# Attention's 64 left rows in full 128-partition tiles, in a kernel of linear attention and two MLPs

## The chip, the cores and the metric

The kernel runs on one core of one Trainium2 chip. The metric is the device time of one execution in microseconds (us); less is better. Matrix products and transpositions run on TensorE (PE; the loading of its stationary operand is shown as PEld), elementwise work on VectorE (DVE), ScalarE (ACT) and GpSimd (POOL), and SyncE (SP) issues most of the DMAs.

## The reference

Linear attention with a norm, then two MLPs on its output; all in float32 (the weights of the MLPs come as float64):

```python
kv  = einsum('bhsd,bhse->bhde', k, v)        # batch 4, heads 8, s 576, d 64
o   = einsum('bhsd,bhde->bhse', q, kv)
o   = o / sqrt(mean(o*o, -1) + 1e-6) * g_norm
x   = o.transpose(0, 2, 1, 3).reshape(2304, 512)
x   = softplus(x @ w_in)  @ w_out            # 512 -> 2048 -> 512
out = leaky_relu(x @ w_in2, 0.01) @ w_out2
```

## The kernel before, in words

**Units.** Attention is done in 16 units, one for two heads of one batch (4 batches, 4 pairs of heads). A batch has 576 rows, which are four full tiles of 128 partitions and 64 left rows. The full rows are loaded by unit (`load`, L363 to L373, five buffers deep), the left rows of all heads once for each batch (L377) into tiles of 64 partitions, `ldr`.

**One unit.** `T` (L383 to L429): GpSimd (in two cases another engine) repacks q and k (`copy_to`, L338); PE transposes the four q tiles (L400) and the left q rows (L404, 64 partitions, `ident[:RL, :RL]`) into PSUM, which is copied to `qt`, whose columns are 128, 128, 64 (left), 128, 128. PE then sums k-transposed times v over the four full tiles (L408) and the left rows (L411, contraction over 64 partitions); VectorE multiplies this with a mask into `kvm` (L426). `O` (L433 to L454): PE multiplies the four full tiles of `qt` with `kvm` (L439) and the 64 left columns (L445, an output of 64 partitions in `ps[6]`), and ACT and DVE take the sums of squares. For every second unit `normal` (L469 to L506) forms the norm and writes `xn` and, for the left rows, `xnl`. `X` (L517 to L545) transposes `xn` (L523) and, once for two units, `xnl` (L535, 64 partitions) and writes the result, scaled, to `xy`, the x of the MLPs.

A product in float32 is two passes on PE (two pairs of a weight load and a matmul in the trace), a transposition one.

**Order.** Nothing is issued in the order of the source: each piece of work is an `op` with a cost for each engine that may do it, with the buffers that it reads and writes, and `Plan.run` (L91 to L150) puts them into one fixed order for each engine from these costs and due times. The engines then work through their orders, each waiting by semaphores. The costs of PE in the plan are 0.25 for each half of the transpositions of q, 1.1 for kv, 0.87 and 0.22 for the two parts of `O`, 0.44 and 0.11 for those of `X`. The change leaves all of them.

**The MLPs** follow. Their first products (L888) stand among attention's last units; the rest (L813, L961, L977) fill the time behind attention. The decoding of the weights (L576 to L594) and their splitting (L610 to L669) for them is spread over ACT and DVE, during attention too.

Of the kernel before, what the change touches and what calls it, by code (L numbers as in the profile page):

```python
# [131 lines left out]
def linear_attention_two_mlps(  # L132
# [32 lines left out]
    nc = tc.nc  # L165
    B, H, S, D = q.shape
    NT, DM = out.shape
    DFF = w1.shape[1] // 2
    P = 128
    KC = DM // P  # L170
    NF = DFF // P
    RL = S - 4 * P
# [29 lines left out]
    def ring(pool, name, n, shape, dt=F32):  # L202
        return [pool.tile(shape, dt, name=f"{name}{i}") for i in range(n)]

    ident = const.tile([P, P], F32, name="ident")
# [91 lines left out]
    ps = ring(psum, "ps", 8, [P, 512])  # L297
# [3 lines left out]
    mstp = mst.__enter__()  # L301
    att = tc.tile_pool(name="att", bufs=1)
    attp = att.__enter__()
    NLD = 5
    lda = {nm: ring(attp, nm + "a", NLD, [P, 2, 4, D]) for nm in "qkv"}
    ldr = {nm: ring(attp, nm + "r", 2, [RL, H, D]) for nm in "qkv"}
    qp = ring(attp, "qp", 2, [P, 4, 2, D])
    kp = ring(attp, "kp", 2, [P, 4, 2, D])
    qt = ring(attp, "qt", 2, [P, S])
    kvm = ring(attp, "kvm", 2, [P, P])  # L310
    sq = ring(mstp, "sq", 2, [P, 8, D])
    sql = ring(mstp, "sql", 1, [RL, 4, D])
    xn = ring(mstp, "xn", 4, [P, 8, D])
    xnl = ring(mstp, "xnl", 2, [RL, 4, D])

    ss = ring(mstp, "ss", 2, [P, 20])
    fa = ring(mstp, "fa", 2, [P, 20])
    fm = ring(mstp, "fm", 2, [P, 20])
    for t_ in ss:
        nc.vector.memset(t_, 1.0)  # L320

    plan = Plan()
    op = plan.op
# [39 lines left out]
    def load(u):  # L363
        b, hp = u // NPAIR, u % NPAIR
        hs = slice(2 * hp, 2 * hp + 2)
        for nm, src in (("q", q), ("k", k), ("v", v)):
            def fn(e, nm=nm, src=src):
                nc.sync.dma_start(  # L368
                    out=lda[nm][u % NLD],
                    in_=src[b, hs, 0:4 * P, :].rearrange("h (p r) d -> p h r d", r=4),  # L370
                )

            op({"S": 0.73}, fn, (), [(nm, u % NLD)])  # L373
        if hp == 0:
            for nm, src in (("q", q), ("k", k), ("v", v)):
                def fn(e, nm=nm, src=src):
                    nc.sync.dma_start(  # L377
                        out=ldr[nm][b % 2], in_=src[b, :, 4 * P:S, :].rearrange("h p d -> p h d")
                    )

                op({"S": 0.73}, fn, (), [(nm + "r", b % 2)])

    def T(u):  # L383
        b, hp = u // NPAIR, u % NPAIR
        h2 = slice(2 * hp, 2 * hp + 2)
        i = u % 2
        for nm, dst in (("q", qp), ("k", kp)):
            copy_to(
                dst[i], lda[nm][u % NLD].rearrange("p h r d -> p r h d"), 512,
                [(nm, u % NLD)], [(nm + "p", i)],  # L390
            )
        p0 = 2 * i if u < U_H else 0
        p1 = p0 + 1
        kv = ps[p1][:, 2 * P:3 * P]
        ql, kl, vl = (ldr[nm][b % 2] for nm in "qkv")
        va = lda["v"][u % NLD]

        def f_t(e, j):
            for r in range(2):
                nc.tensor.transpose(  # L400
                    ps[p0 + j][:, r * P:(r + 1) * P], qp[i][:, 2 * j + r, :, :], ident
                )
            if j == 0:
                nc.tensor.transpose(ps[p0][:, 2 * P:2 * P + RL], ql[:, h2, :], ident[:RL, :RL])  # L404

        def f_kv(e):
            for r in range(4):
                nc.tensor.matmul(  # L408
                    kv, kp[i][:, r, :, :], va[:, :, r, :], start=(r == 0), stop=False
                )  # L410
            nc.tensor.matmul(kv, kl[:, h2, :], vl[:, h2, :], start=False, stop=True)  # L411

        for j in range(2):
            n = (2 * P + RL, 2 * P)[j]
            c0 = (0, 2 * P + RL)[j]
            op(
                {"PE": 0.25}, lambda e, j=j: f_t(e, j),
                [("qp", i)] + ([] if j else [("qr", b % 2)]), [("ps", p0 + j)],
            )
            if j:  # L420
                op(
                    {"PE": 1.1}, f_kv,
                    [("kp", i), ("v", u % NLD), ("kr", b % 2), ("vr", b % 2)], [("ps", p1)],
                )
                op(
                    {"D": 0.22}, lambda e: nc.vector.tensor_tensor(kvm[i], kv, mask, ALU.mult),  # L426
                    [], [("ps", p1), ("kvm", i)],
                )
            from_psum(qt[i][:, c0:c0 + n], ps[p0 + j][:, :n], n, p0 + j, [("qt", i, j)])  # L429
# [3 lines left out]
    def O(u):  # L433
        i = u % 2
        at_ = (0, P, 2 * P + RL, 3 * P + RL)

        def f_o(e):
            for r in range(4):
                nc.tensor.matmul(  # L439
                    ps[4 + i][:, r * P:(r + 1) * P], qt[i][:, at_[r]:at_[r] + P], kvm[i],  # L440
                    start=True, stop=True,
                )

        def f_l(e):
            nc.tensor.matmul(  # L445
                ps[6][:RL, i * P:(i + 1) * P], qt[i][:, 2 * P:2 * P + RL], kvm[i],
                start=True, stop=True,
            )

        need = [("kvm", i), ("qt", i, 0)]  # L450
        op({"PE": 0.87}, f_o, need + [("qt", i, 1)], [("ps", 4 + i)])
        op({"PE": 0.22}, f_l, need, [("ps", 6)])
        squares(ps[4 + i], ("ps", 4 + i), sq[i], ss[u // 2 % 2][:, 8 * i:8 * i + 8], ("sq", i),
                ("ss", u // 2 % 2, i), P, 8)  # L454
# [14 lines left out]
    def normal(w):  # L469
        i = w % 2  # L470
        s_, a_, m_ = ss[i], fa[i], fm[i]
        mk = [("fm", i)]
        sk, ak = [("ss", i, t) for t in range(3)], [("fa", i)]
        ol = ps[6][:RL, 0:2 * P]
        squares(ol, ("ps", 6), sql[0], s_[:RL, 16:20], ("sql", 0), sk[2], RL, 4)
        op(
            {"A": 0.2},
            lambda e: nc.scalar.activation(
                a_, s_, AF.Ln, bias=eps_b, scale=2.0 ** -SHIFT / D
            ), sk, ak,  # L480
        )
        op(
            {"A": 0.2},
            lambda e: nc.scalar.activation(a_, a_, AF.Exp, bias=ln_b, scale=-0.5),
            ak, ak + [("set", 0)],
        )

        def newton(e):
            nc.vector.scalar_tensor_tensor(m_, s_, D * EPS, a_, ALU.add, ALU.mult)
            nc.vector.scalar_tensor_tensor(m_, m_, 1.0 / D, a_, ALU.mult, ALU.mult)  # L490
            nc.vector.scalar_tensor_tensor(m_, m_, -3.0, a_, ALU.add, ALU.mult)

        op({"D": 0.55}, newton, sk + ak, mk)
        parts = [
            (xn[2 * i + t], ps[4 + t], m_[:, 8 * t:8 * t + 8], ("ps", 4 + t), ("xn", 2 * i + t), P, 8)
            for t in range(2)
        ] + [(xnl[i], ol, m_[:RL, 16:20], ("ps", 6), ("xnl", i), RL, 4)]
        for x_, o, r_, ok, xk, p, n in parts:
            op(
                {"D": t_d(n * D)},  # L500
                lambda e, x_=x_, o=o, r_=r_, p=p, n=n: nc.vector.tensor_tensor(
                    x_, o.rearrange("p (g d) -> p g d", d=D),
                    r_[:, :, None].to_broadcast([p, n, D]), ALU.mult,
                ),
                mk, [ok, xk],
            )  # L506
# [10 lines left out]
    def X(u):  # L517
        b, hp = u // NPAIR, u % NPAIR
        i = u % 2

        def f_x(e):
            for r in range(4):
                nc.tensor.transpose(  # L523
                    ps[7][:, r * P:(r + 1) * P], xn[u % 4][:, 2 * r:2 * r + 2, :], ident
                )

        cm, cl = (b * S + RL, b * S) if b % 2 else (b * S, b * S + 4 * P)
        op({"PE": 0.44}, f_x, [("xn", u % 4)], [("ps", 7)])
        scaled(xy[:, hp, cm:cm + 4 * P], ps[7], 4 * P, 7, xyk([hp], cm, 4 * P))
        if i == 0:  # L530
            return

        def f_l(e):
            for t in range(2):
                nc.tensor.transpose(  # L535
                    ps[6][:, 2 * P + t * RL:2 * P + (t + 1) * RL],
                    xnl[u // 2 % 2][:, 2 * t:2 * t + 2, :], ident[:RL, :RL],
                )

        op({"PE": 0.11}, f_l, [("xnl", u // 2 % 2)], [("ps", 6)])  # L540
        scaled(
            xy[:, hp - 1:hp + 1, cl:cl + RL],
            ps[6][:, 2 * P:2 * P + 2 * RL].rearrange("p (a n) -> p a n", a=2),
            2 * RL, 6, xyk([hp - 1, hp], cl, RL),
        )  # L545

# [473 lines left out]
    for t in range(2):  # L1020
        op(
            {"S": 0.1},
            lambda e, t=t: nc.sync.dma_start(
                out=graw[t * D:(t + 1) * D, :], in_=g_norm.rearrange("(p o) -> p o", o=1)
            ),
# [40 lines left out]
    for s in range(2 * NT2 + 2):  # L1066
        t, u = s // 2, s % 2
# [84 lines left out]
```

## Time and profile before

| | us |
|---|---|
| median of 3 runs (lowest, highest) | 844.09 (843.69, 844.68) |
| the profiled execution: its own time | 841.17 |
| its span, first to last instruction | 839.4 |
| PE busy / DVE busy / ACT busy / POOL busy | 824.8 / 578.1 / 447.8 / 65.6 |

The profile is one execution. Its rows give the start of a piece of work from the start of the span in us, its length, the engine, the line of the kernel, and what it reads and writes. "x8" is eight instructions in one row. PE's matmuls are pipelined: the busy time of one overlaps that of the next, so the distance at which they follow one another is read from the chain of waits, whose pieces lie end to end. Attention takes about the first 93 us of the span; the MLPs have the rest.

### The profile page before, as it was taken

The numbers are of one execution on the slowest core, as the hardware profiler recorded it, in microseconds if no ns is written. First come the engines' busy times: TensorE is split into PE (matmuls) and PEld (weight loads), VectorE is DVE, ScalarE is ACT, GpSimd is POOL, SyncE is SP. The second block draws the span as 40 slices with busy tenths as digits, with TensorE's granted clock in tenths as the row PEclk, the third lists the DMA queues.
The fourth block names the chain that finished last, engine by engine and source line by source line (L and its number), as shares of the span: only waits on it lengthen the run. The fifth ranks groups of instructions, "written<-read, shape, count | busy, mean of one in ns | idle before, by whom it ended". The sixth has DMA issues, their size and how long they took to land.

```text
span 839.4 us, 11949 instructions
## 1 busy us (share of the span) xinstructions
PE 824.8 (98%) x4524; PEld 772.0 (92%) x4524; DVE 578.1 (69%) x928; ACT 447.8 (53%) x725; POOL 65.6 (8%) x116
## 2 busy tenths in 40 slices
PE   6999999999999999999999999999999999999997
PEld 4788999999999999999999988989889889889886
DVE  6887988878468665867688886766378754753342
ACT  4644976866355544555466565565364554453330
POOL 3321000000100100000000000010010010010000
PEclk9999999999999999999999999999999999999999
DMA  9981565376645752764866965764654852543613
GB/s 309 342 271 64 201 244 188 145 251 211 222 135 162 248 204 72 249 202 158 302 209 212 324 252 191 253 221 134 210 168 135 286 176 65 200 152 100 200 51 100
DMA packets 78712, 164.08 MB, mean 195 GB/s; under 512 B 11456, under 2 KB 54208, under 8 KB 78656
## 3 DMA queue, kind: packets, MB, share of 16 engines
q1 hardware_dynamic: 67136, 100.42, 35.7%
q0 software_dynamic: 11520, 62.92, 22.6%
q8 instruction: 35, 0.57, 0.3%
q14 instruction: 21, 0.17, 0.1%
HBM read 132.25 MB, written 31.06 MB: 195 GB/s over the span
## 4 chain that ended last, share of the span: by engine, by line
PE 96%; DVE 1%; DMA 1%; ACT 1%; SPq 0%; issue 0%; ACTq 0%; DVEq 0%
PE ps L813 40%; PE ps L961 24%; PE ps L977 24%; PE ps L439 2%; PE ps L408 2%; PE ps L888 2%; PE ps L400 1%; PE ps L523 1%; DMA qr<-in_q_dram 1%; PE ps L411 1%; PE ps L445 1%; PE ps L404 0%; DVE xy L691 0%; PE ps L535 0%; SPq L368 0%
## 5 line engine op out<-in xcount | busy, mean ns | idle before, releaser
L813 PE MATMUL ps<-ra 128*128 128x384 f32 x1932 | 387.8, 335 | 0.0
L813 PEld LDWEIGHTS ps<-ra 128*128 128x128 f32 x1932 | 342.8, 188 | 14.0
L961 PE MATMUL ps<-rb 128*128 128x384 f32 x1152 | 226.6, 334 | 0.0
L977 PE MATMUL ps<-rb 128*128 128x512 f32 x864 | 224.7, 393 | 0.0
L961 PEld LDWEIGHTS ps<-rb 128*128 128x128 f32 x1152 | 202.1, 188 | 0.0
L921 DVE TENSOR_TENSOR mf<-ps,mf 128x384 f32<-128x384 f32 x138 | 76.7, 556 | 165.6 <-PE ps L813 134.3
L977 PEld LDWEIGHTS ps<-rb 128*128 128x128 f32 x864 | 159.8, 188 | 23.7
L914 ACT ACTIVATE mf<-ps 128x384 f32<-128x384 f32 x138 | 67.8, 492 | 109.4 <-PE ps L813 108.2
L691 DVE TENSOR_TENSOR xy<-ps,xy 128x384 f32<-128x384 f32 (+1 forms) x126 | 77.3, 614 | 29.1 <-PE ps L977 20.8
L796 POOL DMA_DIRECT2D ra<-xscr x80 | 42.8, 536 | 672.3 <-PE ps L813 652.8
L847 DVE TENSOR_TENSOR rb<-mf,rb 128x768 fp32r<-128x768 f32 x96 | 91.3, 951 | 3.9 <-ACT rb L842 3.8
L842 ACT ACTIVATE rb<-mf 128x768 fp32r<-128x768 f32 x96 | 81.3, 847 | 2.7
L719 ACT ACTIVATE ra<-mf 128x768 fp32r<-128x768 f32 x63 | 53.0, 841 | 27.7 <-PE ps L813 26.7
L714 DVE TENSOR_TENSOR ra<-mf,ra 128x768 fp32r<-128x768 f32 x63 | 60.1, 955 | 11.0 <-ACT ra L719 10.7
L834 ACT ACTIVATE mf<-mf 128x768 f32<-128x768 f32 (+1 forms) x48 | 32.8, 683 | 61.6 <-DVE mf L921 61.6
L828 ACT ACTIVATE mf<-mf 128x768 f32<-128x768 f32 (+1 forms) x48 | 33.3, 694 | 45.1 <-DVE mf L921 45.0
L686 ACT ACTIVATE xy<-ps 128x384 f32<-128x384 f32 (+1 forms) x35 | 18.5, 528 | 15.1 <-PE ps L961 10.8
L588 DVE SCALAR_TENSOR_TENSOR sqr<-mf,sqr 128x512 int32<-128x512 int32 x35 | 24.4, 696 | 0.8
L594 DVE SCALAR_TENSOR_TENSOR mf<-mf,sqr 128x512 int32<-128x512 int32 x34 | 24.0, 706 | 0.4
L576 ACT ACTIVATE mf<-mf 128x512 f32<-128x512 f32 x20 | 13.4, 669 | 17.1 <-DMA mf<-in_moe_w_in_dram 13.7
L400 PE MATMUL ps<-ident,qp 128*128 128x128 f32 x64 | 13.3, 306 | 8.6 <-POOL qp L347 7.8
L582 DVE TENSOR_SCALAR sqr<-mf 128x512 int32<-128x512 int32 x34 | 15.4, 453 | 8.1 <-ACT mf L576 7.5
(85 smaller groups left out, 606.6 us busy)
## 6 DMA issues: line engine op xcount, KB each, us to landing
ra<-xscr POOLq DMA_DIRECT2D x80, 768.0 KB, 6.0
mf<-xscr SPq DMA_DIRECT2D x51, 384.0 KB, 5.5
mf<-in_moe_w_in_dram SPq DMA_DIRECT2D x18, 512.0 KB, 4.8
xscr<-ra SPq DMA_DIRECT2D x12, 768.0 KB, 3.8
xscr<-rc SPq DMA_DIRECT2D x12, 768.0 KB, 4.6
mf<-in_moe_w_out_dram SPq DMA_DIRECT2D x17, 512.0 KB, 4.3
lf<-in_moe_w_out_dram SPq DMA_DIRECT2D x15, 512.0 KB, 3.5
xscr<-xy SPq DMA_DIRECT2D x19, 384.0 KB, 4.1
```

The lines of the kernel that those rows point to most:

```text
L691: {"D": t_d(n)}, lambda e: nc.vector.tensor_tensor(dst, src, dst, ALU.add),
L714: ENG[e].tensor_tensor(e_[:, 1, :, :], src(), e_[:, 0, :, :].bitcast(F32), ALU.subtract)
L719: {"A": t_a(n)}, lambda e: nc.scalar.activation(e_[:, 0, :, :], src(), AF.Copy),
L796: lambda e: nc.gpsimd.dma_start(out=flat(xe[i]).ap, in_=xscr[7 * tp + i]),
L813: nc.tensor.matmul(o, w_[:, a, c:c + P], e_[:, b, kk, :], start=(not on and kk == 0 and n == 0), stop=(kk == 1 and n == 2), skip_group_che ...
L828: {"A": t_a(n)}, lambda e: nc.scalar.activation(dst(), src(), AF.Softplus),
L842: {"A": t_a(n)}, lambda e: nc.scalar.activation(g[:, 0, :, :], c.ap, AF.Copy),
L847: lambda e: nc.vector.tensor_tensor(g[:, 1, :, :], c.ap, g[:, 0, :, :].bitcast(F32), ALU.subtract),
L914: {"A": t_a(BN)}, lambda e: nc.scalar.activation(c[:, m, :], src, AF.Copy),
L921: lambda e: nc.vector.tensor_tensor(c[:, m, :], src, c[:, m, :], ALU.add),
L961: nc.tensor.matmul(y[:, :BN], w_[m][:, a, js], G_[:, b, m, :], start=(u == 0 and m == 0 and i == 0), stop=(u == 1 and m == 1 and i == 2),)
L977: nc.tensor.matmul(y, G_[:, a, m, js], w_[m][:, b, :], start=(u == 0 and m == 0 and i == 0), stop=(u == 1 and m == 1 and i == 2),)
```

## The change

The tiles of the left rows (`ldr` for q, k, v, and `xnl`) get 128 partitions instead of 64. The lower 64 are set to zero once, ahead of everything else, by eight memsets on VectorE; the DMAs and the norm write the upper 64 as before. The transposition of the left q rows, the kv product of the left rows and the transposition of `xnl` take all 128 partitions. The left product of `O` takes 128 columns of `qt` (the 64 left ones and the first 64 of the next tile) and writes 128 partitions of `ps[6]`, of which 64 are read; for this it needs the second half of `qt` too. The copies out of PSUM take the same elements as before.

```diff
-    ldr = {nm: ring(attp, nm + "r", 2, [RL, H, D]) for nm in "qkv"}
+    ldr = {nm: ring(attp, nm + "r", 2, [P, H, D]) for nm in "qkv"}
...
-    xnl = ring(mstp, "xnl", 2, [RL, 4, D])
+    xnl = ring(mstp, "xnl", 2, [P, 4, D])
...
+    for t_ in [t for n in "qkv" for t in ldr[n]] + xnl:
+        nc.vector.memset(t_[RL:], 0.0)
     for t_ in ss:
         nc.vector.memset(t_, 1.0)
...
-                        out=ldr[nm][b % 2], in_=src[b, :, 4 * P:S, :].rearrange("h p d -> p h d")
+                        out=ldr[nm][b % 2][:RL], in_=src[b, :, 4 * P:S, :].rearrange("h p d -> p h d")
...
-                nc.tensor.transpose(ps[p0][:, 2 * P:2 * P + RL], ql[:, h2, :], ident[:RL, :RL])
+                nc.tensor.transpose(ps[p0][:, 2 * P:3 * P], ql[:, h2, :], ident)
...
-                ps[6][:RL, i * P:(i + 1) * P], qt[i][:, 2 * P:2 * P + RL], kvm[i],
+                ps[6][:, i * P:(i + 1) * P], qt[i][:, 2 * P:3 * P], kvm[i],
...
-        need = [("kvm", i), ("qt", i, 0)]
-        op({"PE": 0.87}, f_o, need + [("qt", i, 1)], [("ps", 4 + i)])
+        need = [("kvm", i), ("qt", i, 0), ("qt", i, 1)]
+        op({"PE": 0.87}, f_o, need, [("ps", 4 + i)])
         op({"PE": 0.22}, f_l, need, [("ps", 6)])
...
-        ] + [(xnl[i], ol, m_[:RL, 16:20], ("ps", 6), ("xnl", i), RL, 4)]
+        ] + [(xnl[i][:RL], ol, m_[:RL, 16:20], ("ps", 6), ("xnl", i), RL, 4)]
...
-                    ps[6][:, 2 * P + t * RL:2 * P + (t + 1) * RL],
-                    xnl[u // 2 % 2][:, 2 * t:2 * t + 2, :], ident[:RL, :RL],
+                    ps[6][:, (2 + t) * P:(3 + t) * P], xnl[u // 2 % 2][:, 2 * t:2 * t + 2, :], ident,
...
-            ps[6][:, 2 * P:2 * P + 2 * RL].rearrange("p (a n) -> p a n", a=2),
+            ps[6][:, 2 * P:4 * P].rearrange("p (a n) -> p a n", a=2)[:, :, :RL],
```

## Rows read from the trace of the kernel before

**Rows 1.** The page, the chain that ended last, shares of the span by engine.
```profile
PE 96%; DVE 1%; DMA 1%; ACT 1%; SPq 0%; issue 0%; ACTq 0%; DVEq 0%
```

**Rows 2.** Busy time by stretch: from:to, length, then each engine's busy us.
```profile
9.30:24.30 15.00, 14.74 (x81) 11.71 (x81) 11.50 (x26) 6.10 (x12) 4.87 (x8) 1.00 1.12 349
24.30:52.20 27.90, 27.05 (x189) 21.80 (x189) 23.79 (x52) 18.04 (x39) 9.18 (x14) 1.00 1.07 338
52.20:97.30 45.10, 44.80 (x297) 38.90 (x298) 36.77 (x75) 26.89 (x54) 5.72 (x7) 1.00 0.31 104
97.30:110.00 12.70, 12.70 (x75) 12.70 (x75) 12.26 (x16) 11.49 (x21) 0.00 (x0) 1.00 1.02 409
```

**Rows 3.** The chain of waits, 64 to 82 us: start, length, engine and line.
```profile
65.62 1.06 PE ps L888 x6
...
68.90 0.89 PE ps L408 x8
69.79 0.41 PE ps L411 x2
70.20 0.37 PE ps L400 x2
70.57 0.20 PE ps L404
70.78 1.27 PE ps L888 x6
72.05 0.22 PE ps L400 x2
...
74.05 0.27 PE ps L535 x2
74.32 1.09 PE ps L408 x8
...
76.41 0.58 PE ps L445 x4
76.99 1.25 PE ps L888 x6
```

**Rows 4.** Weight loads by line and shape, 0 to 97.2 us: count | busy us, mean ns.
```profile
L439 PEld LDWEIGHTS ps<-kvm,qt 128*128 128x128 f32 x128 | 15.2, 191 | 1.3 <-DVE xn L501 0.7 <-issue 0.2
L400 PEld LDWEIGHTS ps<-ident,qp 128*128 128x128 f32 x64 | 7.6, 150 | 10.7 <-POOL qp L347 7.8 <-issue 0.9 <-ACT qt L356 0.6
...
L411 PEld LDWEIGHTS ps<-vr,kr 64*128 64x128 f32 x32 | 4.9, 192 | 2.0 <-issue 0.2
L445 PEld LDWEIGHTS ps<-kvm,qt 128*64 128x64 f32 x32 | 3.2, 135 | 1.9 <-issue 0.8 <-ACT xy L511 0.5
L404 PEld LDWEIGHTS ps<-ident,qr 64*128 64x128 f32 x16 | 2.3, 141 | 3.4 <-issue 2.7 <-DMA qr<-in_q_dram 0.7
L535 PEld LDWEIGHTS ps<-ident,xnl 64*128 64x128 f32 x16 | 1.6, 137 | 1.1 <-DVE mf L752 0.2 <-issue 0.2
```

**Rows 5.** The same stretches, the instructions of L411 alone (PE, then PEld).
```profile
9.30:24.30 15.00, 2.25 (x8) 1.38 (x8) 1.00 1.12 349
24.30:52.20 27.90, 3.40 (x14) 2.06 (x14) 1.00 1.07 338
52.20:97.30 45.10, 2.43 (x10) 1.47 (x10) 1.00 0.31 104
```

**Rows 6.** What POOL's repacking of q waited for, 27 to 90 us: total, times, longest.
```profile
POOL qp L347 <- PE ps L400: 26.1, 9, 6.1
```

**Rows 7.** VectorE's memsets by line and shape: count | busy us, mean ns.
```profile
L208 DVE MEMSET mask<- 128x128 f32 x1 | 0.2, 165 | 0.8 <-PEq L1134 0.8
...
L320 DVE MEMSET ss<- 128x20 f32 x2 | 0.1, 75 | 0.0
```

**Rows 8.** The start in order of time: SP's first left load, VectorE's first decoding.
```profile
3.46 0.74 SPq L377 DMA_DIRECT2D qr<-in_q_dram  x1
...
5.43 0.43 DVE L582 TENSOR_SCALAR sqr<-mf 128x512 int32<-128x512 int32 x1 [3.92 <-ACT mf L576]
```

## The prediction

> **What bounds the kernel now.** I read the chain of waits first: 96% of it is PE [rows 1], so what leaves PE's order can leave the time, unless another engine then holds PE up. Next the busy time by stretch, because the change touches attention alone, the first 93 us. PE looks full in each stretch, but pipelined matmuls look full at any pace; the column to watch is DVE, the busiest of the others: 11.50 of 15.0 us in the first stretch, 23.79 of 27.9 in the second, 36.77 of 45.1 in the third [rows 2]. From 97.3 us on PE has no idle time, so a gain made before reaches the end, and a loss too. In that stretch DVE is at 12.26 of 12.70 us, 97%, with PE never waiting: a dense order on DVE is possible where its inputs lie ready [rows 2].
>
> Then the chain of waits inside attention, where the pieces on PE lie end to end, so that their lengths are what each step really costs [rows 3]. Eight passes of L408 in full shape take 0.89 us, and two transpositions 0.22: 0.11 a pass. Each row of 64 partitions or columns is longer, and so is the row **behind** it. The same six passes of L888 take 1.06 us behind a full-shaped transposition and 1.27 behind L404. L408's eight take 1.09 instead of 0.89 behind L535. The reader is to see that the left rows cost more than their own time: PE pays going into another shape and coming out of it.
>
> **The change part by part.** *PE, removed.* A visit to a shape of 64 has a price made of its own row less the same passes at 0.11, and of the row behind it less that row's undisturbed length, all from [rows 3]:
> - L404: 0.20 − 0.11 = 0.09, and 0.15 to 0.21 behind it (two transpositions at 0.37 instead of 0.22 as behind L411, or L888 at 1.27 instead of 1.06); I take 0.18. 16 visits [rows 4] at 0.27: 4.3 us.
> - L411: 0.41 − 0.22 = 0.19, and 0.15 behind it. 32 passes in 16 visits [rows 4] at 0.34: 5.4 us.
> - L445: 0.58 − 0.44 = 0.14, and 1.25 − 1.06 = 0.19 behind it. Its 32 passes [rows 4] come in twos and fours, so in 8 to 16 visits; I take 11, nearer to the fours that the row shows, at 0.33: 3.6 us.
> - L535: 0.27 − 0.22 = 0.05, and 1.09 − 0.89 = 0.20. 16 passes in 8 visits [rows 4] at 0.25: 2.0 us.
>
> The sum is 15.3 us of PE's order. That is the most the change can give.
>
> *PE, added.* The passes keep their number. The full shape loads 128 columns for L445 instead of 64: a load of L439 takes 191 ns, one of L445 135 [rows 4]. In full-shaped runs loads of that length follow at 0.11 us a pass, being overlapped [rows 3], so I cost this at nothing; without that cover it is 32 × 56 ns = 1.8 us. For the 32 left transpositions the loads are 150 ns in full shape (L400) against 141 and 137 [rows 4]: at most 0.3 us, hidden alike.
>
> The Trainium skill, "TensorE: Matmul & The Clock Gate", section "LDWEIGHTS (loading the stationary operand)", says that a weight load's time goes by its columns and not by the contraction rows, so that zeros below save nothing and 64 more columns cost, an estimate from its formula, 53 ns. By that rule alone the sum would be a loss, the slower rival below; it says nothing of the row behind, where [rows 3] show most of the price.
>
> *DVE, added.* Eight memsets at the start: six of 64 × 512 and two of 64 × 256. 128 elements took 165 ns and 20 took 75 [rows 7], 0.83 ns an element, so about 0.49 and 0.28 us: 3.5 us. DVE is idle for 3.92 us before its first decoding at 5.43 [rows 8], waiting for ACT and that for a DMA; this hides them. From the far side, 512 elements cost at most four times 165 ns, 0.66 us: 4.6 us in all, 0.7 too late. I take nothing. The first load of left rows leaves SP at 3.46 [rows 8]; if it has to wait for the memset of its tile, all the loads behind it on SP wait too, but q's two tiles are zeroed first, by about 2.5 us.
>
> *A wait added.* L445 now needs the second half of `qt`. Behind it on PE stand L439 or the next transpositions, and ACT's squares wait for it. L439 of the same unit needs that half anyway, so only where L445 led is there a cost, at most its own run, 0.58 us [rows 3]; taken as nothing. DMAs, copies out of PSUM and every cost in the plan stay, so the order stays nearly the same: the one new wait may shift a few pieces, by no row of this trace more than such a run.
>
> *What is late next.* The 15.3 us lie across attention as L411's passes do, 8, 14 and 10 by stretch [rows 5]: 3.8, 6.7 and 4.8 us. As PE advances, DVE must do the same work in less time. I allow it 95%, just under the 97% of its densest stretch [rows 2]. First stretch: 15.0 − 11.50/0.95 = 2.9 us of room; moreover the units there start as their loads land, so half of it, 1.5. Second: 27.9 − 23.79/0.95 = 2.9, less than PE's 6.7, so 2.9. Third: 45.1 − 36.77/0.95 = 6.4, more than 4.8, so 4.8. Loads are no limit from the second stretch on: between 27 and 90 us POOL's repacking of q waited nine times, 26.1 us, for PE to free its buffer [rows 6]. ACT has 9 to 18 us of room in each stretch [rows 2].
>
> **Sum:** 1.5 + 2.9 + 4.8 = 9.2 us. The profiled execution would go from 841.17 (span 839.4 and 1.8 around it) to 832.0. It lay 2.9 below the median of the runs, 844.09; against that I predict **834.9 us**.
>
> **The rivals.**
> 1. *PE alone decides* (DVE's idle time was all waiting for PE, and its order closes up as in the stretch behind 97.3). For it: DVE's share is under 86% everywhere in attention. Against it: 15.3 us out of the 88 from 9.3 to 97.3 would put DVE's 72.06 us [rows 2] at 99%. It gives 844.09 − 15.3 = 828.8.
> 2. *DVE becomes the bound at once*: its waits are for chains (squares on ACT, sum on DVE, norm, the next product), and it gets no denser than in its second stretch, 85%. Then the first gives (15.0 − 13.5)/2 = 0.7, the second nothing, the third 45.1 − 43.3 = 1.8: 2.5 us, 841.6. For it: the norm of two units must be done before PSUM's banks take the next. Against it: the 97% behind attention.
> 3. *No change that shows*: the long rows behind L404 and L411 come from waits and not from shapes. Against it: the same lengths, 0.15 and 0.19 to 0.21, behind four different lines [rows 3]. 844.1.
> 4. *Slower*: the added columns lie open, and going in and out of the shape isn't saved. The place is the passes of L445 and the left transpositions; the price is 1.8 + 0.3 = 2.1 us: 846.2. It decides only if padded passes follow at over 0.11 us and the rows behind keep their length. For it: the loads' means [rows 4]. Against it: L408 and L400 in full shape at 0.11.
>
> **How the numbers follow.** My forecast with DVE between the two rivals' densities, a gain of 6 to 12.5 us (831.6 to 838.1): 0.57. PE alone, above 12.5: 0.12. DVE at once, 1.7 to 6: 0.20. No change: 0.07. Slower: 0.04. A measurement of this kernel can tell about 0.2%, 1.7 us, from no change; so faster 0.89, same 0.07, slower 0.04. The range goes from the price of PE alone to that of DVE at once, 829.0 to 841.5. It leaves out the last two cases and a part of PE alone, some 15 in 100.
>
> **What would show it.** Right: L404, L411, L445 and L535 at 0.11 us a pass in the chain, and L888's six at 1.06 behind all of them; DVE over 90% busy in attention; a few waits of PE for DVE that weren't there; the MLPs' last hundreds of us as long as before, begun some 9 us earlier. Wrong in the size: PE's waits in attention small (rival 1), or some 12 us of them (rival 2). Wrong in the mechanism: rows of 0.37 and 1.27 still standing behind the left rows. Wrong in the cover: the first decoding on DVE later than 5.43.

## The result, and the profile after

The changed kernel takes 831.28 us (median of 4, 830.48 to 832.59) against 844.20 (median of 4): a ratio of 0.9849, 95% interval 0.9831 to 0.9866, some 12.7 us. Once more, in a later set of runs (below, `after_again`), it took 832.26 against 843.43: 0.9884 (0.986 to 0.9909), 9.8 us by the ratio and 11.2 by the medians. Faster beyond the interval, as forecast, and by more than the 9.2 us of the sum; 834.9 was predicted in a range of 829.0 to 841.5. The ratios here are not those of the two medians, and differ from them by up to 0.2%. Single executions of the kernel before spread from 840.2 to 845.5 us in the later runs. The four of the first set (843.69 to 844.68) all lie in the upper half of that, so its 12.7 us is probably at the high end; the profiled one, 841.17, lies low, and the two profiles (841.17 and 830.69) differ by 10.5 us. A second profile of the changed kernel (`after_again`) reaches its first L816 at 88.07 us, 9.4 ahead of the kernel before's 97.47.

The code after has its lines moved by three or four: L404 became L408, L411 L415, L445 L449, L535 L539 (the left rows); L400 L404, L408 L412, L439 L443, L523 L527 (the full ones); L888 L891 and L813 L816 (the MLPs).

The chain of waits of the changed kernel, 64 to 76 us (start, length, engine and line), answers to [rows 3]:

```profile
65.83 0.22 PE ps L539 x2
66.05 0.89 PE ps L412 x8
66.95 0.22 PE ps L415 x2
...
67.61 0.45 PE ps L449 x4
68.05 1.05 PE ps L891 x6
69.10 0.22 PE ps L404 x2
69.32 0.11 PE ps L408
69.43 0.22 PE ps L404 x2
```

Each left row now costs 0.11 us a pass, and each row behind one has its undisturbed length: L412's eight 0.89 behind L539 (1.09 before), L891's six 1.05 behind L449 (1.25), the transpositions 0.22 behind L408. Going into the shape of 64 and out of it is gone.

Where it was gained is read from three places in the same view: the products L439 or L443 of the second pair of units, those of the fifth pair, and the first L813 or L816, with which the part of the MLPs that follows attention begins. Before:

```profile
24.31 2.05 PE ps L439 x16
52.18 2.05 PE ps L439 x16
97.47 1.04 PE ps L813 x6
```

After:

```profile
21.32 2.05 PE ps L443 x16
46.16 2.05 PE ps L443 x16
87.03 1.04 PE ps L816 x6
```

3.0 us are gained up to the first place (the start differs between executions, see the last section), 3.0 more to the second, 4.4 more to the third: 10.4 in all. From there to the end nothing is gained or lost: 839.4 − 97.47 = 741.9 us and 828.9 − 87.03 = 741.9.

What PE waited for, 8 to 100 us (total, times, longest), before:

```profile
PE ps L400 <- ACT qt L356: 0.7, 2, 0.4
PE ps L439 <- DVE xn L501: 0.4, 2, 0.3
PE ps L404 <- DMA qr<-in_q_dram: 0.3, 1, 0.3
PE ps L523 <- ACT xy L511: 0.2, 1, 0.2
```

and after:

```profile
PE ps L443 <- DVE xn L505: 1.7, 3, 0.8
PE ps L404 <- ACT qt L360: 1.6, 3, 0.8
PE ps L527 <- ACT xy L515: 0.5, 1, 0.5
PE ps L404 <- DVE qt L362: 0.4, 2, 0.2
```

(Left out in both is the first wait, of 7.8 and 7.9 us, for the first repacked q.) These waits went from 1.6 to 4.2 us: 2.6 us came back as waiting for the norm and for copies out of PSUM. With the 10.4 us that the same two profiles differ by, 13.0 of the 15.3 us are accounted for. The other 2.3 aren't; a part may be that the first row behind a wait is itself longer (sixteen passes of L443 take 2.05 us at 46.16, behind a wait, and 1.79 at 55.35).

Busy time by stretch, the columns as in [rows 2]:

```profile
9.30:24.30 15.00, 14.04 (x107) 13.31 (x107) 14.40 (x31) 7.41 (x15) 5.74 (x9) 1.00 1.12 356
24.30:52.20 27.90, 25.49 (x213) 23.85 (x212) 25.52 (x56) 20.05 (x45) 10.63 (x15) 1.00 1.05 332
52.20:97.30 45.10, 44.03 (x311) 43.07 (x311) 41.09 (x78) 32.86 (x64) 4.97 (x6) 1.00 0.54 195
```

DVE is at 14.40 of 15.00 in the first stretch, 96%, and at 91% in the others. These are the same times, not the same work. Between the three places, which bound the same work, DVE's share went from 85% to 94% (23.46 of 24.84 us) and from 82% to 89% (36.48 of 40.87). In the chain that ended last its share rose from 1% [rows 1] to 4%.

### The profile page after: what moved, and what is told of

Same layout as the page of the kernel before. It is cut to its first block, busy times and chain, and to the rows that moved or that the text cites. A ratio compares the mean times of both kernels' runs of the same rounds, so it can differ in the third digit from the quotient of the medians.

```text
span 828.9 us, 11958 instructions
## 1 busy us (share of the span) xinstructions
PE 811.5 (98%) x4524; PEld 769.6 (93%) x4524; DVE 581.0 (70%) x936; ACT 447.4 (54%) x725; POOL 67.3 (8%) x116
## 4 chain that ended last, share of the span: by engine, by line
PE 93%; DVE 4%; ACT 1%; DMA 1%; issue 0%; POOL 0%; SPq 0%; ACTq 0%; DVEq 0%
PE ps L816 41%; PE ps L964 24%; PE ps L980 24%; PE ps L891 1%; PE ps L443 1%; DMA qa<-in_q_dram 1%; PE ps L412 1%; DVE ra L660 1%; DVE ss L468 1%; PE ps L527 1%; DVE mf L639 0%; PE ps L404 0%; DVE xn L505 0%; DVE fm L494 0%; ACT ra L656 0%
## 5 line engine op out<-in xcount | busy, mean ns | idle before, releaser
L816 PE MATMUL ps<-ra 128*128 128x384 f32 x1932 | 387.8, 335 | 0.0
L816 PEld LDWEIGHTS ps<-ra 128*128 128x128 f32 x1932 | 342.8, 188 | 14.0
L689 ACT ACTIVATE xy<-ps 128x384 f32<-128x384 f32 (+1 forms) x35 | 18.5, 527 | 15.3 <-PE ps L964 11.4
L404 PE MATMUL ps<-ident,qp 128*128 128x128 f32 x64 | 12.4, 297 | 10.0 <-POOL qp L351 7.9
L597 DVE SCALAR_TENSOR_TENSOR lf<-lf,sqr 128x512 int32<-128x512 int32 x30 | 20.6, 686 | 0.4
```

The lines of the kernel that those rows point to most:

```text
L597: lambda e: nc.vector.scalar_tensor_tensor(a_reg.ap, a_reg.ap, -(1 << 31), t_, ALU.bitwise_and, ALU.bitwise_or), tk + ak, ak,
L816: nc.tensor.matmul(o, w_[:, a, c:c + P], e_[:, b, kk, :], start=(not on and kk == 0 and n == 0), stop=(kk == 1 and n == 2), skip_group_che ...
```

## The experiments

All times are medians beside the kernel before in the same runs: 843.49 in the first set of four, 843.62 in the second, 843.43 in the third.

**The four parts, each alone.**

```diff
only_q:
-    ldr = {nm: ring(attp, nm + "r", 2, [RL, H, D]) for nm in "qkv"}
+    ldr = {nm: ring(attp, nm + "r", 2, [P if nm in "q" else RL, H, D]) for nm in "qkv"}
...
+    for t_ in ldr["q"]:
+        nc.vector.memset(t_[RL:], 0.0)
...
-                nc.tensor.transpose(ps[p0][:, 2 * P:2 * P + RL], ql[:, h2, :], ident[:RL, :RL])
+                nc.tensor.transpose(ps[p0][:, 2 * P:3 * P], ql[:, h2, :], ident)
only_kv:
+    ldr = {nm: ring(attp, nm + "r", 2, [P if nm in "kv" else RL, H, D]) for nm in "qkv"}
...
+    for t_ in ldr["k"] + ldr["v"]:
+        nc.vector.memset(t_[RL:], 0.0)
only_o:
-                ps[6][:RL, i * P:(i + 1) * P], qt[i][:, 2 * P:2 * P + RL], kvm[i],
+                ps[6][:, i * P:(i + 1) * P], qt[i][:, 2 * P:3 * P], kvm[i],
...
+        need = [("kvm", i), ("qt", i, 0), ("qt", i, 1)]
only_x:
+    xnl = ring(mstp, "xnl", 2, [P, 4, D])
...
+    for t_ in xnl:
+        nc.vector.memset(t_[RL:], 0.0)
...
+                    ps[6][:, (2 + t) * P:(3 + t) * P], xnl[u // 2 % 2][:, 2 * t:2 * t + 2, :], ident,
...
```

The lines that these replace, and those that keep the DMAs, the norm and the copy out of PSUM at their 64 rows, are as in the change.

> The kernel before with one part of the change: q's left rows in full tiles (two memsets, the DMA into the upper half, L404 with 128 partitions and 128 columns). Theory A (each visit to the 64 shape has a price on PE, and the prices add): L404's 16 visits cost 4.3 us, of which attention keeps 60 to 100%: a gain of 2.5 to 4.5 us; in the chain L404 is 0.11 and the row behind it has its undisturbed length, while L411, L445 and L535 keep theirs. Rival B (the gain of the whole change comes from the new order that L445's added wait gives): within 1 us of before.

839.35 us, ratio 0.9949 (0.9933 to 0.9965): 4.3 us.

> The kernel before with one part of the change: k's and v's left rows in full tiles (four memsets, L411 with a contraction over 128 partitions). Theory A: 16 visits cost 5.4 us of PE's order, so a gain of 3 to 5.5 us; L411's two passes take 0.22 in the chain instead of 0.41. Rival B: within 1 us of before. Rival C (zeros in the contraction save nothing, since a pass takes as long with 64 rows as with 128): L411 stays at 0.41 and the time too.

837.59 us, ratio 0.9929 (0.9911 to 0.9947): 6.0 us. Its chain of waits shows the one part mended beside the others (here L402 and L406 are the full and left transpositions, L410 and L413 the full and left products of kv, L890 the MLP's):

```profile
65.82 0.89 PE ps L410 x8
66.72 0.22 PE ps L413 x2
66.94 0.22 PE ps L402 x2
67.16 0.20 PE ps L406
67.36 1.25 PE ps L890 x6
```

The left product takes 0.22 (0.41 before) and the transpositions behind it 0.22 (0.37), while the left transposition is still at 0.20 with 1.25 behind it. No pass and no column was taken away here: only zeros were added to the contraction.

> The kernel before with one part of the change: L445 with 128 columns of qt, and its wait for the second half of qt. Theory A: 11 visits cost 3.6 us, so a gain of 2 to 3.7 us. Rival B: nearly the whole gain of the change, 10 us or more. Rival C (more columns cost): slower by up to 1.8 us, since each of 32 weight loads is 56 ns longer.

842.36 us, ratio 0.9987 (0.9974 to 1.0001): 1.1 us, which the interval doesn't tell from nothing; the gain lies below what theory A expected. It excludes rival B's 10 us, and a loss of 1.8.

> The kernel before with one part of the change: xnl in full tiles (two memsets, L535 with 128 partitions). Theory A: 8 visits cost 2.0 us, so a gain of 1 to 2 us. Rival B: within 1 us of before, nearer nothing. If the four single parts add up to more than the whole change gains, something that only the whole change meets (VectorE as the next bound) has taken the rest.

841.68 us, ratio 0.9981 (0.9965 to 0.9996): 1.6 us.

The four add up to 4.3 + 6.0 + 1.1 + 1.6 = 13.0 us, beside 12.7 and 9.8 for the whole change; each of the four is uncertain by over 1 us. The stretch from the second pair's products to the first L813 or L816 (in these kernels L813, L814 or L815), in one profiled execution each, leaves out the noise of the start: 73.2 us before, 71.8 in `only_q` (22.98 to 94.76), 70.4 in `only_kv` (23.10 to 93.47), 71.3 in `only_o` (26.18 to 97.51), 71.6 in `only_x` (24.76 to 96.39): gains of 1.4, 2.8, 1.8 and 1.5, together 7.5. The whole change has 65.7 there, a gain of 7.5, and 66.1 in its second profile. So nothing that only the whole change meets has taken a share of note.

The prices of the visits in this stretch (11 of L404's, 12 of L411's, 9 of L445's, all 8 of L535's) come to 3.0, 4.1, 3.0 and 2.0 us, together some 12. So each part by itself already keeps less than its price there. Most of what is missing lies between the second and the fifth pair: the whole change gained 3.0 there for visits priced at 6.2, and 4.4 behind it for 5.9.

**The added wait alone.**

```diff
-        need = [("kvm", i), ("qt", i, 0)]
+        need = [("kvm", i), ("qt", i, 0), ("qt", i, 1)]
```

> The kernel before with nothing but L445's added wait for the second half of qt, shapes as before. Theory A: within 1 us of before, to either side. Rival B (the gain comes from the new order): a gain of 5 us or more.

842.60 us, ratio 1.0008 (0.9992 to 1.0023). The new order neither gains nor loses that the interval could tell: rival B falls.

**Less work for VectorE, in both kernels.**

```diff
-            lambda e: nc.vector.tensor_reduce(sum_, s_, axis=AX, op=ALU.add), [sk], [mk],
+            lambda e: nc.vector.tensor_reduce(sum_, s_[:, :, :8], axis=AX, op=ALU.add), [sk], [mk],
```

> The kernel before, with the sums of squares taken over 8 of the 64 values of a head, at the same costs in the plan, so in the same order: 24 sums on VectorE are cut, some 0.5 us each for 16 and 0.3 for 8, about 10 us of VectorE's work. The norm is then formed from a part of the squares. Theory A (PE's order bounds attention before, VectorE has room): a gain of 0 to 3 us. Rival D (VectorE is the bound before as well, and the change gained by shortening VectorE's waits): 5 us or more.

844.00 us, ratio 1.0002 (0.9986 to 1.0017): no gain, so VectorE's load didn't bound the kernel before.

> The changed kernel with the same cut of the sums of squares. Theory A (with the shapes gone VectorE is the bound of the first half of attention; PE waits there): a gain over the changed kernel of 3 to 6 us, more than the same cut gives the kernel before, so some 14 to 18 us under before; VectorE's pieces leave the chain between 11 and 40 us. Rival E (the chain of dependences, not VectorE's load, holds PE): under 2 us.

831.49 us, ratio 0.9869 (0.9851 to 0.9888), beside 0.9849 and 0.9884 for the changed kernel itself: none of the 3 to 6 us here either. The cut was made, as the groups by line and shape show; in the changed kernel and then in this one:

```profile
L468 DVE TENSOR_REDUCE ss<-sq 128x8 f32<-128x512 f32 x16 | 10.7, 680 | 0.7 <-ACT sq L463 0.6
```

```profile
L468 DVE TENSOR_REDUCE ss<-sq 128x8 f32<-128x64 f32 x16 | 3.5, 216 | 3.5 <-ACT sq L463 3.3
```

These sums take 7.2 us less, with those of the left rows (3.2 to 1.4 us) 9.0; 2.8 us of it shows as more idle time before the sums. In the stretch from the second pair to the first L816, 65.1 us (22.84 to 87.94) stand instead of 65.7 and 66.1, while VectorE's share between the three places fell from 94% and 89% to 83% and 77%. So it isn't VectorE's load that holds PE after the change; theory A's part on VectorE falls. What is left is rival E, chains in which each engine's order waits on another's; no run here shortens such a chain by itself, so this is argued and not shown. One of them is read in the chain of waits of the changed kernel, 35 to 40 us:

```profile
35.07 1.06 ACT ra L656
36.13 0.21 ACT fa L482
36.34 1.21 DVE ra L660
37.55 0.51 DVE fm L493
38.09 0.56 DVE fm L494
38.67 0.19 DVE fm L495
38.89 0.70 DVE xn L505
...
39.63 1.16 PE ps L443 x8
```

PE's next products wait for the norm (L493 to L505), the norm stands on VectorE behind the splitting of a weight (L660), and this behind ScalarE's part of the same (L656).

**The cover of the memsets.**

```diff
-    for t_ in [t for n in "qkv" for t in ldr[n]] + xnl:
+    for t_ in ([t for n in "qkv" for t in ldr[n]] + xnl) * 2:
```

> The changed kernel with its eight memsets issued twice: 3.8 us more of VectorE at the start, where the cover was 3.9 us and the eight took all of it. Theory A (the first decoding on VectorE then starts at 9.3 instead of 5.5 us, and VectorE is in the chain from 11 us on): 2 to 4 us slower than the changed kernel. Rival F (the start waits for loads, so VectorE's start has room): under 1 us slower.

834.10 us, 2.8 above the changed kernel's first runs, 1.8 above its second, and 2.6 above `slim_after` in the same set, with intervals just apart (0.9889 to 0.9923 against 0.9851 to 0.9888). In the changed kernel the last pair of the eight memsets and the first decoding stand like this in the order of time:

```profile
4.60 0.55 DVE L322 MEMSET xnl<- 64x256 f32 x2
5.19 0.10 DVE L324 MEMSET ss<- 128x20 f32 x2
5.49 0.43 DVE L585 TENSOR_SCALAR sqr<-mf 128x512 int32<-128x512 int32 x1 [0.20 <-ACT mf L579]
```

The 3.92 us of idle time [rows 8] are down to 0.20 and the first decoding starts at 5.49 instead of 5.43: covered, with nothing to spare. Issued twice, they push it to 9.00:

```profile
8.39 0.55 DVE L322 MEMSET xnl<- 64x256 f32 x2
...
9.00 0.83 DVE L585 TENSOR_SCALAR sqr<-mf 128x512 int32<-128x512 int32 x1
```

and 1.8 to 2.8 of these 3.5 us reach the end. Rival F falls.

**What holds the stretch from 24 to 44 us, and a version to keep.** The loads were the next suspect, since in `slim_after` they stand in the chain there.

> The changed kernel once more, on the chip and in the hours of the three that follow, for their comparison and for the spread of its executions. Expected: 831 to 832 us, some 12 us under the kernel before.

832.26 us, ratio 0.9884 (0.986 to 0.9909).

The new argument of `decode_pair` is what the load's op reads in the plan, and in the plan alone: it holds the two loads back until the twelfth unit's `kvm`.

```diff
late_w2:
-                decode_pair(0, 1, 0)
+                decode_pair(0, 1, 0, [("kvm", 1)])
```

> The changed kernel, with the two loads of the second MLP weights that stand among attention's loads (33 and 36 us in its trace) put behind all of attention's loads in the plan, and their decoding with them. Theory G (with the shapes gone the loads of q, k and v bound the stretch from 24 to 44 us, beside VectorE): up to 2 us faster than the changed kernel, since two loads of 1.3 us leave the queue. Theory A alone (VectorE's load): 0 to 1 us, from the decoding that moves. Rival E (chains of dependences): nothing, or a loss where the decoding comes back late.

833.08 us, ratio 0.9889 (0.9865 to 0.9913): no gain. Attention isn't shorter (25.9 us from the second pair, at 21.47, to the fifth, at 47.38, against 24.8), and the first L816 comes later, at 90.33 (87.03 in the changed kernel's first profile, 88.07 in its second), for the decoding now stands near the end of attention.

> Both cuts on the changed kernel: sums of squares over 8 of 64 values (the norm is then formed from a part of the squares) and the two weight loads behind attention's. Alone the shorter sums brought nothing. Theory G (loads and VectorE bind the same stretch, so each hides the other): 1.5 to 4 us faster than the changed kernel, more than the two cuts alone together. Rival E: within 1 us of the changed kernel.

832.77 us, ratio 0.9886 (0.9862 to 0.9910). With both cuts nothing is gained either, so the gain that theory G forecast isn't there. That no load holds this stretch isn't shown by it: two loads of weights were moved and those of q, k and v stayed, and in the chain of `slim_late` one of them still stands:

```profile
22.77 3.65 DMA va<-in_v_dram
```

```diff
late_qt_act:  late_w2, and
-            from_psum(qt[i][:, c0:c0 + n], ps[p0 + j][:, :n], n, p0 + j, [("qt", i, j)])
+            from_psum(qt[i][:, c0:c0 + n], ps[p0 + j][:, :n], n, p0 + j, [("qt", i, j)], "A" if u < U_H else "AD")
```

> A version meant to be kept: the changed kernel with the two weight loads behind attention's, and with all copies of the first ten units' transposed q out of PSUM on ScalarE, which takes some 4 us of copies from VectorE where ScalarE has 8 us of room between 24 and 52 us. Theory G: 1 to 3 us faster than the changed kernel. Rival E: within 1 us, or slower, since ScalarE's copies stand behind its squares in its order and PE waits for them.

831.57 us, ratio 0.9870 (0.9845 to 0.9895), against 0.9884 for the changed kernel in the same set: the intervals overlap, so this is no better version that could be shown. Its one profile has 64.5 us from the second pair to the first L816 (22.17 to 86.67) against 65.7 and 66.1, a hint that copies on VectorE are links of such chains. No run here beats the change beyond the intervals.

## Why the prediction was right, point by point

*What bounds the kernel.* PE's order inside attention, shown: VectorE's work cut by some 9 us left the kernel before where it was (`slim_before`), while taking the shapes out of PE's order gained in each of three parts by itself. Between the second and the fifth pair only half of the price was kept, so there PE's order isn't the only bound.

*The prices.* The rows of the chain were mended as priced, and the visits are as many as were taken: 16, 16, 11 and 8. By the medians L404 at 4.3 us gained 4.3, L411 at 5.4 gained 6.0, L535 at 2.0 gained 1.6, L445 at 3.6 gained 1.1. That they agree is in part chance, for the medians hold the noise of the start; behind the second pair's products the four parts kept 1.4 of 3.0, 2.8 of 4.1, 1.5 of 2.0 and 1.8 of 3.0 us. So the sum of 15.3 is a price in PE's order, not a gain, for each part by itself too. In the one profile of `only_o` the slow passes at the start last longer than in those of the other three parts, up to L439's first eight (2.07 us; 1.16 in `need_only`); whether that is why its median gains least stays open.

*Added columns.* Taken as nothing, rightly. L449's weight loads are as long as foreseen, in the groups by line:

```profile
L415 PEld LDWEIGHTS ps<-vr,kr 128*128 128x128 f32 x32 | 5.0, 199 | 0.0
L449 PEld LDWEIGHTS ps<-kvm,qt 128*128 128x128 f32 x32 | 4.6, 191 | 0.0
```

191 ns instead of 135 [rows 4], hidden behind the passes: L449's four still take 0.45 us in the chain. So the Trainium skill's rule ("TensorE: Matmul & The Clock Gate", section "LDWEIGHTS (loading the stationary operand)") agrees on the load itself, which follows the columns (L415 199 ns with 128 contraction rows, 192 with 64), and the time went the other way: rival 4 fell, and with it the reading that zeros in the contraction save nothing (`only_kv`). The loads' idle time agrees with the chain: just before their loads, 2.0 us for L411 and 1.9 for L445 [rows 4], 0.0 for both after. So a load into another shape stood idle first, which one into the same shape didn't. The Trainium skill, "TensorEngine Tiling (Array Packing)", section "Key Properties", says that changing the tiling mode drains the engine. The rows agree with that: 0.15 to 0.21 us behind each such change [rows 3], gone after it. No row names the mode itself, so that this rule is the cause is argued.

*Memsets, the added wait.* 3.7 us (1.41 to 5.15) against 3.5 estimated, covered; and nothing for the wait (`need_only`).

*What is late next.* This is the step that failed. It let VectorE's density, at most 95%, take 6.1 us of PE's 15.3. The mechanism was wrong: with 9 us less of VectorE's work the changed kernel isn't faster (`slim_after`). What the profiles show in its place is 2.6 us of added waits in chains across engines, and 2.3 us that no row accounts for. The sign set for it, DVE over 90% busy in attention, came true all the same, so it told nothing of the cause. By stretch the profiles gained 3.0, 3.0 and 4.4 us against 1.5, 2.9 and 4.8; the 2.9 of the second was met by a limit of VectorE that isn't there. The first was undervalued, but by less than it looks: between two profiles with like starts (the kernel before and `after_again`, last section) it is 24.31 − 21.96 = 2.35 us. L411's passes were a rough guide to where the price lies, too: by each line's own visits it is 3.4, 6.2 and 5.9 us, not 3.8, 6.7 and 4.8. And "loads are no limit from the second stretch on" no longer holds after the change: between 27 and 90 us GpSimd's repacking of q then waits 5.9 us for loads, five times; whether this reaches PE wasn't shown.

That the time came out near, 3.6 and 2.6 us below 834.9, is in part luck: a deduction of about the right size was made for a wrong reason. "DVE becomes the bound at once" (rival 2) falls with `slim_after`. "PE alone decides" (rival 1) forecast 828.8 us and a gain above 12.5, with a chance of 0.12; the 12.7 us of the first set lies at that border, the 9.8 of the second and the 9.4 and 10.4 between profiles don't. The added waits speak against it: PE's order doesn't close up wholly.

## What to carry to other kernels

Read PE's cost of a small matmul from the row behind it as well as from its own: where shapes of 64 and 128 partitions alternate, each visit to the smaller one cost 0.25 to 0.34 us of PE's order here on top of its passes, and zeros in the unused half were cheaper than the change of shape. Count on less than that in the time, 9.4 to 12.7 us for 51 visits here, since PE then waits elsewhere. Compare kernels behind the place where their starts differ. An engine that is 85 to 96% busy beside the bound isn't the next bound by that alone: cut its work once and see whether the time moves before sums are built on its density. Zeroing that is done once at the start cost nothing here as long as the first real work of its engine waited for a load; of 3.5 us beyond that, 1.8 to 2.8 reached the end.

## What the runs showed of the hardware

Small operations of VectorE were held up by GpSimd's. The norm's pieces of 20 elements take 0.18 us by themselves; where GpSimd repacks q or k they end with GpSimd's instruction. Changed kernel, in order of time, GpSimd's:

```profile
26.46 1.14 POOL L351 TENSOR_SCALAR qp<-qa 128x512 f32<-128x512 f32 x1 [1.89 <-DMA qa<-in_q_dram]
27.57 0.61 POOL L351 TENSOR_SCALAR kp<-ka 128x512 f32<-128x512 f32 x1
```

and VectorE's:

```profile
27.04 0.58 DVE L493 SCALAR_TENSOR_TENSOR fm<-ss,fa 128x20 f32<-128x20 f32 x1
27.66 0.55 DVE L494 SCALAR_TENSOR_TENSOR fm<-fm,fa 128x20 f32<-128x20 f32 x1
28.24 0.18 DVE L495 SCALAR_TENSOR_TENSOR fm<-fm,fa 128x20 f32<-128x20 f32 x1
```

The first ends at 27.62, GpSimd's first at 27.60; the second at 28.21, GpSimd's second at 28.18; the third runs free. The Trainium skill, "SBUF — State Buffer", section "Terms", says that the two engines take turns at a shared pair of ports, each for a whole instruction; these rows agree. A norm in PE's way is so 0.8 us late here (0.58 and 0.55 instead of 0.18 each) without any engine being full. Two of the pieces in the chain at 37.55 and 38.09 us above are such long ones. No run here takes the repacking off GpSimd, so the cause is read from these times alone.

The start isn't the same in each execution: PE's first passes follow at about half the later pace, and for how long differs. The second group of L412's eight took 1.06 us in one profile of the changed kernel and 1.73 in the other (order of time, first and second profile):

```profile
12.79 1.06 PE L412 MATMUL ps<-va,kp 128*128 128x128 f32 x8
```

```profile
13.00 1.73 PE L412 MATMUL ps<-va,kp 128*128 128x128 f32 x8
```

The later places keep the difference and add to it: 21.32 and 21.96 us for the second pair's products, 46.16 and 47.18 for the fifth pair's, 87.03 and 88.07 for the first L816. The kernels with the old shapes spread more. Here are the second group of L408's eight in the chain of the kernel before, of `need_only` and of `slim_before`; the second pair's products begin at 24.31, 25.50 and 23.25:

```profile
13.74 1.76 PE ps L408 x8
13.77 1.99 PE ps L408 x8
13.35 1.09 PE ps L408 x8
```

So much of the spread of single executions seems to be made here; no run shows it for those without a profile. It isn't waiting alone: single instructions are longer too, in the second profile of the changed kernel up to 499 ns for L412's passes and 338 for their weight loads, against medians of 275 and 192. The column of the granted clock reads 1.00, the higher of its levels, over this stretch in both, so it gives no reason, and the cause stays open. Of the 3.0 us that the first stretch gained, part may be this, which is why the sums above are also made behind it.
